# V of one pair of heads moved ahead of a weight tile and held until the first pair is normalised; the order of the early steps written out

## The chip, the cores and the metric

The kernel runs on one core of a Trainium2 chip. The metric is the device time of one execution in microseconds; several executions are timed and their median is given. One further execution is recorded by the hardware profiler; its trace gives the rows below, in microseconds from the start of its span.

The engines are named as in the profile: PE is TensorE, with its weight loads as PEld; DVE is VectorE, ACT is ScalarE, POOL is GpSimd, and SP is SyncE, which issues nearly all transfers.

## The reference

Attention with a local window and some global tokens feeds two MLP stages one after the other:

```python
def _attn_ref(q_l, k_l, v_l, q_g, k_g, v_g):          # (4, 8, 512 or 32, 64) each
    k_all, v_all = [concatenate of global and local]
    s_g = scale * q_g @ k_all^T ; out_g = sm(s_g) @ v_all
    s_ll = scale * q_l @ k_l^T, kept where |i - j| <= 32
    s_lg = scale * q_l @ k_g^T
    out_l = sm([s_lg, s_ll]) @ v_all
    return [out_g, out_l]

x = attention output as (2304, 512)
h = x @ w_in                                           # (512, 2048)
x = (h * clip(h + 3, 0, 6) / 6) @ w_out                # (2048, 512)
h = max(x @ w1, x @ w2, x @ w3)                        # (512, 768) each
out = h @ w_4                                          # (768, 512)
```

All of it is float32. The kernel makes each float32 product from three products of a rounded high part and a low part (`hi`, `lo`).

## The kernel before, in words

Attention is worked in 16 steps of one batch and one pair of heads (`pair(b, pr, s0)`, four batches by four pairs). For one pair the queue of SP loads Q, K and V (`qr`, `kr`, `vr`, three buffers each); TensorE makes the scores (L469), VectorE masks them and takes the row maximum (`rowmax`, L482), ScalarE takes exponentials (L488), TensorE turns them (`flip`, L512), and `pv` (L523) multiplies them with V. `norm` (L531) divides by the sums and writes the tile `ox`; TensorE turns it once more (`xflip`, L538), and ScalarE and VectorE write its high and low parts into `rx` (L550, L552). For every second pair `globals_` does the same for the global tokens (L576 scores, L587 row maximum, L607 flip, L620 product with V).

Beside this run the loads of w_in: 16 tiles of 512 KB go into a staging tile `raw` with two buffers (`decode`, L664). ScalarE and VectorE put the float32 bits together (L642 to L652), and ScalarE and POOL write the high and low parts (L668, L669). With these the first MLP stage, `first` (L695), starts as soon as x of the first two pieces of tokens is there; its tiles are stored to HBM by SP (`gstore`, L721). The second, third and fourth matrix products follow (L859, L983, L1138).

The order of the work on every engine is fixed when the program is built. Each step is an `op` with an engine, an estimated duration, a due time, the buffers it reads and writes, and at times an earliest time `rel`. `Plan.order` plays the steps through against these estimates and takes, on each engine, the ready step with the earliest due time; the instructions are issued in the order in which it took them. [...] In the list of before, SP's transfers around the change are: Q and K of the third pair; V of the second; w_in's first tile; Q and K of the fourth pair; w_in's second tile; V of the third pair; Q and K of the fifth pair; w_in's third tile.

A `Buf` is one use of a buffer, and `Plan.op` makes a step wait for every earlier step that touches the same `Buf` where one of them writes. V's load is issued by line 455 (`v` below). The lines that build the operands of the third product for the tokens "A" (`operands`, L1039) and the sums of the last stage (`double`, L1154) carry the other two due times that the change touches.

Of the kernel before, what the change touches and what calls it, by code (L numbers as in the profile page):

```python
# [33 lines left out]
TOK = {"A": (0, 256), "B": (512, 512), "C": (1536, 320)}  # L34
# [65 lines left out]
class Plan:  # L100
# [40 lines left out]
    def order(self):  # L141
# [4 lines left out]
        free, cand, out, pipe, port, form = {}, {}, [], 0.0, dict(DVE=0.0, POOL=0.0), "F"  # L146
# [22 lines left out]
        def elsewhere(o, e, t):  # L169
            mine = cost(o, e, t)  # L170
            return any(cost(o, x, begin(o, x)) < mine - (0.0 if x < e else 1e-6) for x in o.may if x != e)

        def begin(o, e):
# [18 lines left out]
                    t = max(t, max(u.done for u in old.users) + 0.1)  # L192
            return t

        while len(out) < len(self.ops):
            picks, wait, at = [], {}, {}
            for e, ops in cand.items():
                f = free.get(e, 0.0)
# [2 lines left out]
                    wait[e] = [(o.due, o.n, SHARE * o.may[e] if o.may else o.us) for t, _, o in at[e] if t <= f + LOOK]  # L201
            for e, ops in cand.items():
                ts = [(t, o) for t, b, o in at[e] if not (o.may and elsewhere(o, e, b))]
                if not ts:
                    continue
                if e == "PE":
                    ts = [(t + stall(o, t), o) for t, o in ts]
                t0 = min(t for t, _ in ts)
                stay = lambda o: e == "PE" and form != "F" and FORM.get(o.what) == form
                pick = min(((not stay(o), o.due, o.n, t, o) for t, o in ts if t <= t0 + WAIT), key=lambda x: x[:3])[1:]  # L210
                picks.append((pick[2], e != "-", pick[0], pick[1], pick[3], e))
            assert picks, "no step can start"
            t0 = min(picks)[0]
            t, _, _, _, o, e = min((p for p in picks if p[0] <= t0 + WAIT), key=lambda p: p[1:4])
# [43 lines left out]
                o.end = max([d.end for d in o.deps] + [t])  # L258
            o.done = o.end + (DRAIN if o.eng == "PE" else 0.0)
            cand[o.eng].remove(o)  # L260
            out.append(o)
            for s in o.succ:
                s.left -= 1
# [3 lines left out]
        return out  # L267


PLAN = []  # L270
WAIT = 0.02
RATE = 340.0
# [7 lines left out]
SPLIT = 2  # L280
LATE, SHARED = 2.473, 0.718
TS = "BC"
STEPS = (7.62, 8.87, 11.397, 7.881)
LAG = 124.236
W4DUE = 4
# [10 lines left out]
def body(ctx, tc, q_n, k_n, v_r, w_in, w_o, w_3, w_4, out):  # L296
# [144 lines left out]
    def pair(b, pr, s0):  # L441
# [7 lines left out]
        for n, (t, src, cut, size) in enumerate(((Q, q_n, 256, NQ + SG), (K, k_n, 448, NK))):  # L449
            for i, (a, z) in enumerate(((0, cut), (cut, size)) if first_ else ((0, size),)):  # L450
                e, issue = ("ACT", nc.scalar) if first_ and n else ("SP", nc.sync)
                op(e, 0.45, lambda t=t, src=src, a=a, z=z, issue=issue: issue.dma_start(
                    out=t()[:, a:z], in_=src[b, pr][:, a:z]), s0 - 7.919 + i, w=[(t, i)] if first_ else [t],
                   kb=(z - a) / 2, rel=s0 - 15.079, what="qk"[n])
        op("SP", 0.5, lambda: nc.sync.dma_start(out=V(), in_=v_r[b, pr]), s0 - 4.432 + 5 * first_, w=[V], kb=1024, rel=s0 - 2.826, what="v")

        TB, NM, OB = [Buf(T["t"]) for _ in range(2)], Buf(T["nm"]), Buf(T["o"])
# [67 lines left out]

        op("PE", 0.95, pv, s0 + 3.515, r=PT + [V], w=[OB], what="pv", ni=129)
        OX, XT = Buf(T["ox"]), Buf(T["s"])

        def norm():
            r = NM()[:, 2].rearrange("p i h -> p (i h)").rearrange("p (x o) -> p x o", o=1).to_broadcast([128, 8, D])  # L530
# [145 lines left out]
    def tt(e, out, a, b, f):  # L676
        ENG[e].tensor_tensor(out=out, in0=a, in1=b, op=f)  # L677
# [358 lines left out]
    yb = lambda p: lambda i: yv(p)[:, (1, 3, 0, 2)[i]]  # L1036
    yk = lambda p: [YK[p, i] for i in (1, 3, 0, 2)]
    S = {}
    S["A"] = operands(yb("A"), [Y["A"]], yk("A"), "sA", TOK["A"][1], TD - 14)  # L1039
    S["C"] = operands(yb("C"), [Y["C"]], yk("C"), "sC", TOK["C"][1], TD - 8)  # L1040
    plan.event(lambda: (fw_es.close(), re.open()), ("fw",), ("re",))
    S["B"] = operands(yb("B"), [Y["B"]], yk("B"), "sB", TOK["B"][1], TD + 8)
# [102 lines left out]
    def double(ts, due, t):  # L1145
# [5 lines left out]
                out=blk(2 - 2 * i, 2).rearrange("p (k m) -> p k m", k=NH), in_=hd[:, :, ts[i]:ts[i] + 128]),  # L1151
               t - 12, r=rows(ts[i]), w=[(W, 1 - i)], kb=560, what="hload")
        for o, x, y, f in ((4, 0, 1, ALU.add), (6, 2, 0, ALU.subtract), (5, 4, 2, ALU.subtract), (7, 3, 5, ALU.subtract)):
            op(both(384), dp(384), lambda e, o=o, x=x, y=y, f=f: tt(e, blk(o), blk(x), blk(y), f), t - 7, r=[key(x), key(y)], w=[key(o)],  # L1154
               what="wsum")
        for at, k in ((1, 3), (4, 4)):
            r = [key(i) for i in range(at, at + k)]
# [72 lines left out]
```

## Time and profile before

| | us |
|---|---|
| median of 3 runs | 712.08 |
| lowest, highest | 710.86, 712.6 |
| the profiled execution, device time | 708.55 |
| the profiled execution, span of its instructions | 706.8 |
| TensorE busy in that span | 693.6 |
| VectorE, ScalarE, POOL busy | 528.1, 380.0, 124.7 |

The profile is read from TensorE, which is busy nearly all the time: the list of its waits says where it is not, the table of windows says how busy each engine and the DMA engines are in a stretch and which clock TensorE was granted, and the timeline shows the instructions around one place. The time from 0 to about 160 us is attention with the first MLP stage beside it.

### The profile page before, as it was taken

Reading aid. Unit: us, or ns where it says so; the run is one execution under the profiler, and the core shown is the slowest. Engines: PE = TensorE matmul, PEld = TensorE weight load, DVE = VectorE, ACT = ScalarE, POOL = GpSimd, SP = SyncE. Lnnn points to the kernel's source line nnn. Section 1 sums busy time; section 2 is a strip of 40 time slices with the busy share of each in tenths; the row PEclk is TensorE's granted clock in tenths of the full one; section 3 lists DMA queues with packets and bytes.
Section 4 is the critical chain, followed back from the end, with each engine's and each line's share of the span. In section 5 each row is a group of like instructions: output and inputs, shape, how many; then the busy total and the mean of one; then the engine's idle time right before and its main releaser. Section 6 shows DMA issues by size and latency. Waiting matters only on the chain.

```text
span 706.8 us, 16042 instructions
## 1 busy us (share of the span) xinstructions
PE 693.6 (98%) x6380; PEld 617.2 (87%) x6380; DVE 528.1 (75%) x1117; ACT 380.0 (54%) x807; POOL 124.7 (18%) x161
## 2 busy tenths in 40 slices
PE   7899999999999999999999999999999999999998
PEld 5677888788888999988999998898999999898998
DVE  5798986657863565699867589998878876486980
ACT  6798886754432334565554366755444435154552
POOL 2136463200001352101010000011211320010100
PEclk9999999999999999999999999999999999999999
DMA  9689988716875766675576588001463471366632
GB/s 345 242 319 346 341 337 318 254 62 234 318 267 222 264 229 220 245 244 177 146 234 186 144 293 289 15 1 59 147 218 105 153 239 50 105 193 216 186 130 90
DMA packets 67003, 144.57 MB, mean 205 GB/s; under 512 B 4976, under 2 KB 35440, under 8 KB 63856
## 3 DMA queue, kind: packets, MB, share of 16 engines
q1 hardware_dynamic: 66640, 143.13, 58.6%
q8 instruction: 50, 0.82, 0.5%
q10 hardware_dynamic: 288, 0.41, 0.2%
q14 instruction: 25, 0.20, 0.1%
HBM read 98.04 MB, written 45.48 MB: 203 GB/s over the span
## 4 chain that ended last, share of the span: by engine, by line
PE 90%; DMA 3%; DVE 2%; ACT 2%; issue 1%; SPq 0%; POOL 0%; ACTq 0%; POOLq 0%
PE bank L983 34%; PE bank L695 25%; PE bank L859 22%; DMA kr<-in_kn_dram 2%; PE o L523 2%; PE bank L1138 2%; PE s L512 2%; PE s L469 1%; PE s L538 1%; PE s L620 1%; DMA fw<-gsC 1%; ACT t L488 1%; DMA raw<-in_w_in_dram 1%; PE s L576 1%; PE s L607 1%
## 5 line engine op out<-in xcount | busy, mean ns | idle before, releaser
L695 PE MATMUL bank<-rx,rw 128*128 128x512 f32 (+1 forms) x960 | 197.8, 362 | 0.5 <-DVE rx L552 0.2
L695 PEld LDWEIGHTS bank<-rx,rw 128*128 128x128 f32 x960 | 161.8, 188 | 23.5 <-issue 1.2
L859 PE MATMUL bank<-rr,rw 128*128 128x320 f32 (+2 forms) x912 | 154.7, 331 | 0.9 <-DVE rr L677 0.9
L859 PEld LDWEIGHTS bank<-rr,rw 128*128 128x128 f32 x912 | 140.3, 188 | 14.7 <-DVE rr L677 1.7
L983 PE MATMUL bank<-rw,rr 128*128 128x256 f32 (+2 forms) x648 | 100.0, 302 | 0.1
L983 PEld LDWEIGHTS bank<-rw,rr 128*128 128x128 f32 x648 | 90.5, 188 | 5.0 <-ACT rf L435 0.7
L782 ACT CAST rr<-fw 128x1024 fp32r<-128x1024 f32 (+2 forms) x76 | 62.1, 820 | 53.9 <-PE bank L859 46.3
L677 DVE TENSOR_TENSOR rr<-fw,rr 128x1024 fp32r<-128x1024 f32 (+2 forms) x76 | 72.6, 961 | 23.8 <-ACT rr L782 22.8
L705 ACT ACTIVATE rq<-bank,three 128x512 f32<-128x512 f32 (+1 forms) x60 | 37.9, 635 | 49.9 <-PE bank L695 41.8
L707 DVE SCALAR_TENSOR_TENSOR rq<-rq,bank 128x512 f32<-128x512 f32 (+1 forms) x60 | 36.8, 617 | 30.8 <-ACT rq L705 30.7
L435 ACT COPY rf<-bank 128x256 f32<-128x256 f32 (+2 forms) x72 | 32.9, 465 | 47.9 <-PE bank L983 37.4
L488 ACT ACTIVATE t<-t,nm 128x128 f32<-128x128 f32 x128 | 49.9, 392 | 12.3 <-DVE nm L482 12.1
L677 POOL TENSOR_TENSOR rq<-rq 128x256 f32<-128x256 f32 (+2 forms) x44 | 37.6, 855 | 106.2 <-DVE rq L677 83.1
L677 POOL TENSOR_TENSOR rf<-rf 128x256 f32<-128x256 f32 (+2 forms) x32 | 29.9, 950 | 143.5 <-DVE rf L677 44.2
L983 PE MATMUL bank<-re,rr 128*128 128x512 f32 x222 | 54.9, 391 | 0.0
L983 PE MATMUL bank<-rw,re 128*128 128x256 f32 (+2 forms) x369 | 53.8, 292 | 0.0
L983 PEld LDWEIGHTS bank<-rw,re 128*128 128x128 f32 x369 | 49.3, 188 | 1.6 <-DVE re L677 0.2
L1077 DVE TENSOR_TENSOR rf<-rf,bank 128x320 f32<-128x320 f32 (+2 forms) x72 | 37.0, 529 | 14.8 <-PE bank L983 13.4
L983 PEld LDWEIGHTS bank<-re,rr 128*128 128x128 f32 x222 | 40.7, 188 | 8.0
L482 DVE CUSTOM_DVE_ANT_0 t<-s,mask 128x128 f32<-128x128 f32 x116 | 26.5, 284 | 10.4 <-PE s L469 10.4
L677 DVE TENSOR_TENSOR rf<-rf 128x384 f32<-128x384 f32 (+4 forms) x56 | 30.9, 583 | 3.6 <-DMA rf<-hd 3.5
L677 DVE TENSOR_TENSOR re<-rf,re 128x1024 fp32r<-128x1024 f32 (+4 forms) x20 | 26.5, 1327 | 1.9 <-ACT re L1160 1.9
(134 smaller groups left out, 964.7 us busy)
## 6 DMA issues: line engine op xcount, KB each, us to landing
vr<-in_v_dram SPq DMA_DIRECT2D x16, 1024.0 KB, 7.3
fw<-gsB SPq DMA_DIRECT2D x28, 512.0 KB, 4.7
raw<-in_w_dram SPq DMA_DIRECT2D x24, 512.0 KB, 3.9
fw<-gsC SPq DMA_DIRECT2D x28, 320.0 KB, 3.4
raw<-in_w_in_dram SPq DMA_DIRECT2D x16, 512.0 KB, 5.3
raw<-in_w_o_dram SPq DMA_DIRECT2D x16, 512.0 KB, 4.4
fw<-gsA SPq DMA_DIRECT2D x28, 256.0 KB, 2.8
gsB<-rq SPq DMA_DIRECT2D x6, 1024.0 KB, 5.2
```

The source lines that it names most:

```text
L435: (nc.scalar.copy if eng == "ACT" else nc.vector.tensor_copy)(out=out, in_=in_)
L482: nc.vector.tensor_tensor_reduce(out=TB[hh]()[:, i], in0=SB[hh]()[:, 128 * i:128 * i + 128], in1=mask()[:, (i + 1) // 2 if i < 3 else 2], ...
L488: nc.scalar.activation(out=t, in_=t, func=ACTF.Exp, scale=-1.0, bias=NM()[:, 0, i, hh:hh + 1], accum_out=NM()[:, 1, i, hh:hh + 1])
L512: nc.tensor.transpose(FB()[:, 128 * i:128 * i + 128], TB[hh]()[:, i], ident)
L677: ENG[e].tensor_tensor(out=out, in0=a, in1=b, op=f)
L695: nc.tensor.matmul(ps()[:, 0:m], lhsT=w[:, i, k], rhs=xs(c)[:, j, k], start=(k == 0 and s == 0), stop=(k == KC - 1 and s == 2))
L705: op("ACT", us, lambda ps=ps, m=m, out=out: nc.scalar.activation(out=out(), in_=ps()[:, 0:m], func=ACTF.Relu, bias=three), -100, r=[ps], w ...
L707: op("DVE", us, lambda ps=ps, m=m, out=out: nc.vector.scalar_tensor_tensor(out=out(), in0=out(), scalar=6.0, in1=ps()[:, 0:m], op0=ALU.min ...
L782: op("ACT", act(n) + 0.01, lambda: nc.scalar.copy(out=out(0), in_=src()), due, r=r, w=[(w, "hi")], what=what + "_hi")
L859: nc.tensor.matmul(A[e]()[:, 0:n], lhsT=w[:, 2 * fp + f, u, e], rhs=r[:, v, f], start=(seed is None and fp + f + s == 0), stop=(fp == 3 an ...
L983: nc.tensor.matmul(bank()[:, 0:n], lhsT=w[:, u, k], rhs=r[:, v, k], start=(start and k + s == 0), stop=(k == K - 1 and s == 2), skip_group ...
L1077: op("DVE", dve(n), lambda q=q, src=src, mv=mv: nc.vector.tensor_tensor(out=mv(q)(), in0=mv(q)(), in1=src(), op=ALU.max), -200, r=[bank], ...
```

## The change

V of the third pair (batch 0, pair 2) moves ahead of w_in's second tile in SP's order. Before it stands a new step on POOL, "hold": it copies one column of the first pair's normalised tile `ox` into the first column of that V's buffer. The load of V writes the same buffer, so it waits for the copy, and the copy waits for the first pair's `norm`.

The order of the first 312 steps of TensorE and the first 117 of SP is no longer chosen by due time but given as a list, `SEQ`, of step numbers (a step's number is its place in the order in which the code creates the steps). The other engines are still ordered by `Plan.order`. Against the order of before, the lists hold the same steps; neighbours change places in many spots. Among them: the first pair's two halves of Q (7 before 6), K ahead of Q for the fifth and some later pairs, the third pair's `xflip` ahead of the first `first` step, and the scores that ran at 58.32 before behind four further steps. The due times of the "A" operands and of the last stage's sums move by 4 and 2 us in the planner's time.

```diff
@@ Plan.order
+        turn = {e: list(seq) for e, seq in SEQ.items()}
...
             for e, ops in cand.items():
                 ts = [(t, o) for t, b, o in at[e] if not (o.may and elsewhere(o, e, b))]
+                if turn.get(e):
+                    ts = [(t, o) for t, o in ts if o.n == turn[e][0]]
...
             cand[o.eng].remove(o)
+            if turn.get(o.eng):
+                turn[o.eng].pop(0)
...
+SEQ = dict(
+    PE=(2, 0, 3, 1, 5, 4, 11, 12, 21, 44, 32, 73, 76, 34, 63, 36, 65, 94, 81, 38, 67, 83, 113, 69, 85, 441, 444, 87,
+        115, 125, 117, 119, 265, 266, 144, 412, 271, 267, 146, 272, 273, 148, 431, 433, 449, 451, 150, 461, 453, 268,
...
+    SP=(7, 6, 41, 42, 10, 90, 91, 43, 153, 122, 123, 93, 160, 410, 409, 167, 124, 174, 458, 459, 181, 411, 188, 490,
...
+HOLD = {2: 0}
...
@@ pair
+        if b == 0 and pr in HOLD:
+            was = held[0, HOLD[pr]]["OX"]
+            op("POOL", 0.07, lambda: nc.gpsimd.tensor_copy(out=V()[:, 0, 0, 0:1], in_=was()[:, 0:1]), -100, r=[was], w=[V], what="hold")
         op("SP", 0.5, lambda: nc.sync.dma_start(out=V(), in_=v_r[b, pr]), s0 - 4.432 + 5 * first_, w=[V], kb=1024, rel=s0 - 2.826, what="v")
...
         OX, XT = Buf(T["ox"]), Buf(T["s"])
+        S["OX"] = OX
...
-    S["A"] = operands(yb("A"), [Y["A"]], yk("A"), "sA", TOK["A"][1], TD - 14)
+    S["A"] = operands(yb("A"), [Y["A"]], yk("A"), "sA", TOK["A"][1], TD - 10)
...
@@ double
-            op(both(384), dp(384), lambda e, o=o, x=x, y=y, f=f: tt(e, blk(o), blk(x), blk(y), f), t - 7, r=[key(x), key(y)], w=[key(o)],
+            op(both(384), dp(384), lambda e, o=o, x=x, y=y, f=f: tt(e, blk(o), blk(x), blk(y), f), t - 9, r=[key(x), key(y)], w=[key(o)],
                what="wsum")
```

In the list of SP, 93 is V of the third pair, 160 is w_in's second tile, and 410 and 409 are K and Q of the fifth pair.

## Rows read from the trace of the kernel before

**Rows 1.** The page, part 1: busy us, share of the span, instructions.

```profile
span 706.8 us, 16042 instructions
...
PE 693.6 (98%) x6380; PEld 617.2 (87%) x6380; DVE 528.1 (75%) x1117; ACT 380.0 (54%) x807; POOL 124.7 (18%) x161
```

**Rows 2.** Waits of TensorE, whole span: us in total, times, longest.

```profile
PE s L469 <- DMA kr<-in_kn_dram: 3.1, 3, 1.5
PE o L523 <- issue: 2.9, 2, 2.4
...
PE bank L859 <- DVE rr L677: 0.9, 3, 0.5
PE s L620 <- issue: 0.7, 1, 0.7
```

**Rows 3.** Windows: length, busy PE PEld DVE ACT POOL, granted clock, DMA share, GB/s.

```profile
18.00:20.00 2.00, 0.00 (x0) 0.00 (x0) 0.10 (x1) 2.00 (x10) 0.00 (x0) 0.91 0.98 399
20.00:22.00 2.00, 1.84 (x21) 1.66 (x22) 1.13 (x4) 0.03 (x1) 0.00 (x0) 0.50 0.85 324
22.00:24.00 2.00, 2.00 (x56) 1.58 (x56) 1.03 (x3) 0.86 (x3) 0.00 (x0) 0.73 0.14 53
24.00:26.00 2.00, 1.96 (x19) 1.28 (x17) 1.99 (x7) 1.94 (x7) 0.20 (x1) 1.00 0.00 0
```

**Rows 4.** Timeline, PE: start, us, line, tiles, count, [idle before, releaser].

```profile
13.94 0.30 PE L523 MATMUL o<-vr,pt 128*32 128x64 f32 x2 [0.47 <-issue]
...
16.82 0.91 PE L523 MATMUL o<-vr,pt 128*32 128x64 f32 x49
20.16 0.65 PE L523 MATMUL o<-vr,pt 128*32 128x64 f32 x15 [2.43 <-issue]
...
26.30 1.10 PE L469 MATMUL s<-kr,qr 64*32 64x96 f32 x62 [0.33 <-DVE g L587]
...
28.35 0.73 PE L695 MATMUL bank<-rx,rw 128*128 128x512 f32 x2
...
30.01 0.66 PE L538 MATMUL s<-ident,ox 128*128 128x128 f32 x4 [0.21 <-DVE ox L531]
```

**Rows 5.** DMA queue "instruction", 17.60:17.80, then 21.40:21.60: packets, MB, share of 16 engines.

```profile
q8 instruction: 1, 0.02, 34.2%
...
q8 instruction: 1, 0.02, 31.2%
```

**Rows 6.** Timeline, SP's queue: when transfers were issued.

```profile
11.57 1.41 SPq L664 DMA_DIRECT2D raw<-in_w_in_dram  x1
13.03 0.43 SPq L455 DMA_DIRECT2D vr<-in_v_dram  x1
...
26.92 0.33 SPq L664 DMA_DIRECT2D raw<-in_w_in_dram  x1
```

**Rows 7.** Tile raw: issue to landing of w_in's first (4.85), then third tile (26.92).

```profile
DMA to landing us min/median/max: 11.5/11.5/11.5
...
DMA to landing us min/median/max: 3.8/3.8/3.8
```

**Rows 8.** Timeline, DVE, POOL and ACT around the first and second pair.

```profile
14.28 0.69 DVE L531 TENSOR_TENSOR ox<-o,nm 128x512 f32<-128x512 f32 x1 [0.96 <-PE o L523]
14.32 0.19 POOL L595 TENSOR_TENSOR g<-g,small 128x1 f32<-128x1 f32 x1 [1.26 <-ACT tg L593]
17.02 0.21 POOL L562 MEMSET tg<- 128x128 f32 x1 [2.50 <-PE s L607]
24.02 1.24 ACT L646 ACTIVATE rq<-raw 128x512 f32<-128x512 f32 x2
```

**Rows 9.** Timeline, PE: scores that waited for K, and the next flip.

```profile
7.94 1.10 PE L469 MATMUL s<-kr,qr 64*32 64x96 f32 x64 [1.52 <-DMA kr<-in_kn_dram]
...
58.32 1.10 PE L469 MATMUL s<-kr,qr 64*32 64x96 f32 x64 [1.32 <-DMA kr<-in_kn_dram]
...
60.15 0.60 PE L512 MATMUL s<-ident,t 128*128 128x128 f32 x4
```

18 rows, old and new, of tables (PE, SP) are left out of this document.

## Prediction

> **What bounds the kernel now.** The page first: TensorE is busy for 693.6 of 706.8 us [rows 1]. So the end comes earlier only where TensorE's idle time, or time at a lower clock, disappears. The list of its waits comes next: hardly anything but K tiles that land late (3.1 us), 0.9 us behind splits for the second MLP stage, and two entries "issue", 2.9 and 0.7 us, in which it waited for nothing that has a semaphore [rows 2]. The long one stands in the timeline of TensorE: the second pair's `pv` stops after 49 matmuls at 17.73 and goes on at 20.16; the first pair's had stopped after 62 of 64, for 0.47 us [rows 4]. Between the two stops lie six rows with 2 + 4 + 64 + 4 + 4 + 49 = 127 matmuls, each with its weight load: 254 instructions. The queue named "instruction" moves packets of 0.02 MB; one starts at 17.6 to 17.8, another at 21.4 to 21.6 [rows 5]. I read this as TensorE's own code arriving block by block, the next block being asked for when a block is entered. The packet at 17.7 was then asked for at 13.94 (3.7 us of queueing), and matmuls ran on 2.5 us after it began. The one at 21.5 was asked for at 20.16 (1.3 us).
>
> The windows show what it queued behind and what the stop cost: the DMA engines are full until about 22.0 (0.85 of 20 to 22, 0.14 of 22 to 24, none of 24 to 26), and the granted clock is 0.50 and 0.73 in the two windows after the stop, against 1.00 from 24 [rows 3]. So the load on the DMA engines is 8.0 us deep at 13.94 and 1.8 us at 20.16. The line through the two points is: queueing = 1.3 + 0.39 x (depth - 1.8).
>
> **The change part by part.** *The hold.* POOL gets one copy of 128x1. The nearest row, an addition of that shape, took 0.19 us. The copy waits for the first pair's `norm`, which ends at 14.28 + 0.69 = 14.97, so it ends near 15.2, and V of the third pair is issued near 15.3 instead of 13.03 [rows 6, 8]. Behind the copy on POOL stands the memset of `tg`, which starts at 17.02, when TensorE's global flip releases it [rows 8]: nothing is delayed. Behind V on SP stand, in the new list, w_in's second tile (11.57 before; near 15.8 now) and then K and Q of the fifth pair, which followed V before as well (from 13.56 to near 16.3) [rows 6]. So four transfers, 1024 + 512 + 400 + 288 KB = 2.28 MB, are no longer queued at 13.94. At 399 GB/s [rows 3] that is 5.7 us of depth: 2.3 instead of 8.0. Queueing is then 1.5 us, the packet starts at 15.4, before the held transfers bring data, and matmuls can go on at 17.9 against a stop at 17.73: a stall of **0.2 instead of 2.43 us, 2.2 gained**.
>
> *The clock.* [...] TensorE was busy 1.84 us at 0.50 and 2.00 us at 0.73 [rows 3]; at 1.00 the same work takes 0.92 and 1.46, so 3.84 - 2.38 = **1.46 gained**. The ends of this term are nothing (the clock falls anyway) and 1.46; I take the upper one, since the same rows show 1.00 wherever no such stop came before.
>
> *What is late next.* After 20.16 TensorE runs into VectorE, which has to go from the second pair's `norm` through the second `g_rowmax` (L587) before the fourth pair's scores go on at 26.30 [rows 4]. VectorE idles in 18 to 24 (0.10, 1.13, 1.03 us busy of 2 each [rows 3]), so it can start as much earlier as TensorE does: 2.2 + 1.46 = **3.65 us** at 26.3, which puts that point at 22.65. The next code block: entered at 17.9 with 2.28 MB issued at 15.3 to 16.7. w_in's third tile, issued at 26.92 into an idle queue, landed after 3.8 us [rows 6, 7], 1.3 of which are its 0.52 MB at 399 GB/s; half of the other 2.5 lies before its data, so I let the held data flow from 16.5. At 17.9 0.6 MB of it is through, 4.2 us are left, queueing is 1.3 + 0.39 x 2.4 = 2.2, and the code is there at 17.9 + 2.2 + 2.5 = 22.6. It is needed 127 matmuls further on; the nine rows from 20.16 to 25.61 hold 92, so that is 35 matmuls into the row at 26.30, about 26.9 before and 23.3 now [rows 4, 5]. No new stall, with 0.7 us to spare.
>
> *Who needs the held tiles.* The third pair's `pv` ran at 27.3, the fifth pair's scores later still; issued near 15.3 and 16.3 they land by 23 to 24. The second w_in tile was first read in ScalarE's row at 24.02 (its second instruction, 24.6) [rows 8]. The tile took 3.8 us to land into an empty queue (the third tile) and 11.5 us behind two V (the first) [rows 7]; mine has one V of 2.6 us ahead of it: 15.8 + 3.8 + 2.6 = 22.2. In the shifted timeline it is wanted from 21 on; ScalarE and VectorE have other steps to put there, since their order follows the planner's own times. I take 0, and 2.6 us at worst (below).
>
> *The written list.* It holds the first 312 TensorE and 117 SP steps; compared with the order before, it swaps neighbours. Four swaps have a row. (1) The first pair's Q comes second half first, so the first scores start up to 0.45 us (one issue) later; the cover is the wait of 1.52 us for the second pair's K at 7.94 [rows 9]; cost 0, without the cover 0.45. (2) The third pair's transposition follows its `pv` directly; before, `first` matmuls stood between, from 28.35 to 30.01, and it still waited 0.21 us for VectorE [rows 4]. Between 0 and 30.01 - 28.35 - 0.21 = 1.4 us lost; I take **0.4 lost**, nearer to 0, since VectorE and not TensorE is full there and the skipped work can be done as soon as its weights are decoded. (3) The scores that waited 1.32 us for K at 58.32 go behind one `first` step, a flip and two global flips [rows 9]. The gain is at most 1.3; that flip ran at 60.15, 1.8 us after the scores, so as much can be lost too. I take 0. (4) Halves of `first` and loads change places up to 150 us; the second code stall, 0.7 us [rows 2], can go or come again: 0, plus or minus 0.75.
>
> *The two due times* (A's operands 4 us later, the sums of the last stage 2 us earlier in the planner's ranking): no wait of TensorE after the second MLP stage's 0.9 us is listed [rows 2]. So nothing can be gained; a reordered operand could cost, bounded by a wait of the length listed, 0.5. I take 0.
>
> **Sum.** 2.2 + 1.46 - 0.4 = 3.2 us. From the early stage on TensorE is filled, so the shift reaches the end. The profiled execution, 708.55, would be 705.3; the median of the runs is 712.08, 3.5 above it, and the same shift gives **708.9**. The forecast's own range: 3.65 + 1.3 + 0.75 less nothing gives 706.4; 2.2 - 1.4 - 0.45 gives 711.7.
>
> **Rivals.** *A: the stall moves.* The held transfers crowd the next code block instead. With the full depth of 5.7 us in front, queueing is 2.8 and not 2.2, which the 0.7 us still cover; beyond that each microsecond that the code is late is a microsecond of stop. At the 3.7 us of queueing that the first deep queue showed, the code is there at 24.1, 0.8 late, and if the clock falls behind this stop as it did before, the 1.46 is gone too: 3.2 - 0.8 - 1.46 = 0.9 gained, **711.2**. For: 2.28 MB now lies together. Against: the margin worked out above.
>
> *B: the stop is not made by the queue.* If code waits for one packet in its way at most, emptying the queue gives nothing: **712.1**. For: the first stop, 0.47 us, came with a deep queue too. Against: 3.7 against 1.3 us in two rows that differ in depth.
>
> [...]
>
> *C: slower.* w_in's second tile comes too late. Place: ScalarE's scale of the second tile and VectorE's steps behind it, which stand in order before the fourth pair's rowmax. If the tile takes the first tile's 11.5 us [rows 7] from 15.8, it lands at 27.3, 2.7 us after its first read before, and the whole early stage hangs on it: 712.1 + 2.6 = **714.7**. It decides against the change from a landing after about 24.6; up to there the gain only shrinks. Against: fewer bytes lie ahead of it than of the first tile.
>
> **Chances.** Forecast 0.58, A 0.15, B 0.13, C 0.14. What a measurement of this kernel can tell from no change is about 0.3%, 2.1 us, so faster means below 709.9. Of the forecast 0.50 lies there and 0.08 within; of A 0.03 and 0.12; B is within; of C 0.13 is slower, 0.01 within. Faster 0.53, same 0.34, slower 0.13. The range from 706.3 to 712.5 holds the forecast's own ends, A and B, with the runs' scatter of about 0.4 beyond B, and leaves C out.
>
> **What would show it.** In the profile of after: V of the third pair issued near 15.3, the second w_in tile right behind it; the "instruction" packet near 15.4; the second pair's `pv` with no stop over 0.5 us; a granted clock of 1.00 from 18 to 24; the fourth pair's scores near 22.7; no "issue" wait near 23; and the remaining timeline shifted by some 3 us. Wrong if the packet still starts near 17.6 (B), if a stop of 1 us or more stands near 23 (A), or if ScalarE or VectorE waits for `raw` before 25 (C).

## The result, and the profile after

The changed kernel took 714.57 us (median of 6 runs, 713.32 to 715.85) against 712.19 of the kernel before in the same comparison (6 runs): a ratio of 1.0054, 95% interval 1.0029 to 1.0078, so slower by half a per cent. Run again, instruction for instruction the same, it gave 1.0077 (1.005 to 1.0103). The forecast was 708.9 us, between 706.3 and 712.5.

Line numbers of the changed kernel are higher by 28 to 32: the scores L469 are L500 there, `flip` L512 is L543, `pv` L523 is L554, `xflip` L538 is L570, `first` L695 is L727. The page of the changed kernel, part 1, to hold against [rows 1]:

```profile
span 712.9 us, 16035 instructions
...
PE 698.1 (98%) x6380; PEld 616.4 (86%) x6380; DVE 531.5 (75%) x1109; ACT 381.6 (54%) x811; POOL 130.1 (18%) x166
```

The early part went as forecast. TensorE's timeline, changed kernel, for [rows 4]:

```profile
14.38 1.41 PE L554 MATMUL o<-vr,pt 128*32 128x64 f32 x64
...
18.36 1.43 PE L554 MATMUL o<-vr,pt 128*32 128x64 f32 x64
...
24.53 1.56 PE L500 MATMUL s<-kr,qr 64*32 64x96 f32 x62 [0.16 <-DVE g L619]
26.02 1.10 PE L554 MATMUL o<-vr,pt 128*32 128x64 f32 x64
27.97 0.66 PE L570 MATMUL s<-ident,ox 128*128 128x128 f32 x4 [0.85 <-DVE ox L563]
```

Both `pv` run through, 64 matmuls each with no stop. The second starts 1.54 us later than before and the fourth pair's scores go on 1.77 us earlier: 3.31 us are gained in between, where 3.65 were forecast. The head of this execution, which the change hardly touches, was the slower one (last section). The hold and what it lets go, in the timelines of POOL and SP, for [rows 6]:

```profile
16.61 0.18 POOL L485 COPY vr<-ox 128x1 f32<-128x1 f32 x1 [0.25 <-DVE ox L563]
```

```profile
16.82 0.33 SPq L486 DMA_DIRECT2D vr<-in_v_dram  x1
17.20 1.11 SPq L696 DMA_DIRECT2D raw<-in_w_in_dram  x1
```

And the windows, for [rows 3], with the granted clock at 1.00 in all of them:

```profile
18.00:20.00 2.00, 1.91 (x71) 1.49 (x70) 2.00 (x14) 2.00 (x10) 0.21 (x1) 1.00 0.79 302
20.00:22.00 2.00, 1.74 (x50) 1.33 (x52) 1.72 (x4) 2.00 (x8) 0.00 (x0) 1.00 0.97 387
22.00:24.00 2.00, 2.00 (x41) 1.46 (x29) 1.84 (x6) 1.40 (x6) 0.20 (x1) 1.00 1.01 391
```

The loss comes later. These are the times in the timelines at which the `pv` of some of the 16 pairs starts, and the end of the span. "Before again" and "hold alone" are runs of the next section.

| us | pair 2 | 3 | 5 | 8 | 9 | 10 | 16 | span |
|---|---|---|---|---|---|---|---|---|
| before | 16.82 | 27.32 | 42.81 | 74.01 | 83.47 | 94.91 | 151.81 | 706.8 |
| before again | 18.05 | 29.31 | 45.58 | 76.55 | 86.01 | 97.49 | 155.67 | 710.0 |
| hold alone (second run) | 17.48 | 24.87 | 41.32 | 71.33 | 80.79 | 92.23 | 151.51 | 705.4 |
| changed | 18.36 | 26.02 | 43.13 | 73.46 | 87.62 | 101.64 | 158.06 | 712.9 |
| changed again | 18.82 | 26.23 | 44.79 | 72.17 | 85.98 | 99.96 | 156.41 | 710.8 |

Against before, the changed kernel is 1.3 us ahead at the third pair, 0.3 behind at the fifth and 6.2 behind at the last; 6.1 are left at the end. Against before again it is 2.4 behind at the last and 2.9 at the end, near the 2.4 us between the medians; the first profile of before is a quick execution. (The marks of the second and third pair have the same matmuls before them in both orders. In the list the eighth has 73 fewer before it, the fifth 8, the ninth 44 and the last 48 more, so these marks are off by some 3 us one way and 1 or 2 the other; the end is not.) From the last mark to the end all five take 553.9 to 555.0 us, so the loss lies before it. The waits of TensorE from 40 to 100 us, first before, then changed:

```profile
PE s L469 <- DMA kr<-in_kn_dram: 1.3, 1, 1.3
PE bank L695 <- DVE rx L552: 0.2, 1, 0.2
```

```profile
PE s L570 <- DVE g L619: 1.5, 1, 1.5
PE s L660 <- DVE gx L657: 0.9, 1, 0.9
PE s L652 <- ACT pt L463: 0.8, 1, 0.8
PE s L543 <- ACT t L519: 0.8, 1, 0.8
PE s L543 <- DVE nm L513: 0.5, 1, 0.5
PE o L554 <- DVE pt L463: 0.5, 1, 0.5
PE s L500 <- DVE rx L584: 0.4, 1, 0.4
PE bank L727 <- DVE rq L739: 0.2, 1, 0.2
```

That is 1.5 us against 5.6 us (2.0 in before again; 4.6 in changed again, 1.5 of them a stop marked "issue" at 43.99), and the kind has changed: one late K before, eight places at which TensorE stands in front of a step whose VectorE or ScalarE input is not ready. In windows of 20 us TensorE is busy 18.24 and 18.29 where it was busy 20.00 and 20.00 before (19.16 and 20.00 in before again). Before, then changed:

```profile
60.00:80.00 20.00, 20.00 (x333) 16.18 (x332) 17.42 (x62) 18.09 (x55) 10.74 (x14) 1.00 0.97 344
80.00:100.00 20.00, 20.00 (x393) 16.31 (x392) 17.24 (x63) 16.65 (x51) 10.63 (x15) 1.00 0.87 317
...
60.00:80.00 20.00, 18.24 (x373) 13.67 (x372) 15.96 (x61) 14.15 (x46) 8.75 (x11) 1.00 0.80 273
80.00:100.00 20.00, 18.29 (x324) 14.40 (x323) 17.93 (x62) 16.86 (x53) 11.90 (x15) 1.00 0.83 308
```

A second trace of the same thing lies on SP. Its longest wait of 45 to 100 us for POOL's sums, before and changed:

```profile
SPq L721 <- POOL rq L677: 5.3, 2, 3.2
```

```profile
SPq L753 <- POOL rq L709: 14.2, 3, 7.2
```

For 7.2 us SP stands in front of one store, and a w_in tile, the next store, Q, K and V stand behind it. The DMA engines run empty meanwhile (0.25 and 0.03 of 70 to 74, against 0.91 and 0.86 before), and VectorE, which before never waited for w_in in this stretch, now does. Changed kernel, windows and VectorE's waits:

```profile
70.00:72.00 2.00, 2.00 (x14) 1.69 (x12) 1.63 (x7) 1.98 (x7) 1.39 (x3) 1.00 0.25 102
72.00:74.00 2.00, 1.77 (x21) 1.05 (x19) 1.84 (x5) 1.42 (x3) 1.45 (x2) 1.00 0.03 12
```

```profile
DVE raw L676 <- DMA raw<-in_w_in_dram: 3.3, 3, 1.7
```

### The profile page after: what moved, and what is told of

It is laid out like the page before. It is cut to its first block, busy times and chain, and to the rows that moved or that the text cites. A ratio compares the mean times of both kernels' runs of the same rounds, so it can differ in the third digit from the quotient of the medians.

```text
span 712.9 us, 16035 instructions
## 1 busy us (share of the span) xinstructions
PE 698.1 (98%) x6380; PEld 616.4 (86%) x6380; DVE 531.5 (75%) x1109; ACT 381.6 (54%) x811; POOL 130.1 (18%) x166
## 4 chain that ended last, share of the span: by engine, by line
PE 87%; DMA 5%; DVE 4%; ACT 3%; issue 1%; SPq 0%; ACTq 0%
PE bank L1015 33%; PE bank L727 24%; PE bank L891 21%; DMA raw<-in_w_in_dram 3%; PE bank L1170 2%; PE s L500 1%; PE s L543 1%; PE o L554 1%; ACT t L519 1%; PE s L608 1%; DMA fw<-gsC 1%; DMA kr<-in_kn_dram 1%; DVE t L513 1%; DVE raw L676 1%; PE s L570 1%; DVE rr L709 1%
## 5 line engine op out<-in xcount | busy, mean ns | idle before, releaser
L727 PE MATMUL bank<-rx,rw 128*128 128x512 f32 (+1 forms) x960 | 201.3, 363 | 0.4 <-DVE rq L739 0.2
L727 PEld LDWEIGHTS bank<-rx,rw 128*128 128x128 f32 x960 | 161.0, 188 | 23.0 <-issue 1.3
L709 DVE TENSOR_TENSOR rr<-fw,rr 128x1024 fp32r<-128x1024 f32 (+2 forms) x76 | 74.1, 979 | 24.2 <-ACT rr L814 23.2
L709 POOL TENSOR_TENSOR rq<-rq 128x256 f32<-128x256 f32 (+2 forms) x45 | 39.1, 868 | 106.9 <-DMA gsB<-rq 64.3
L709 POOL TENSOR_TENSOR rf<-rf 128x256 f32<-128x256 f32 (+1 forms) x34 | 31.0, 925 | 136.9 <-DMA w4d<-rf 51.0
L1109 DVE TENSOR_TENSOR rf<-rf,bank 128x256 f32<-128x256 f32 (+2 forms) x72 | 37.0, 529 | 14.6 <-PE bank L1015 13.6
L1015 PE MATMUL bank<-rr 128*128 128x320 f32 (+1 forms) x174 | 27.1, 303 | 0.0
```

What stands on the lines that cost most here:

```text
L727: nc.tensor.matmul(ps()[:, 0:m], lhsT=w[:, i, k], rhs=xs(c)[:, j, k], start=(k == 0 and s == 0), stop=(k == KC - 1 and s == 2))
L1015: nc.tensor.matmul(bank()[:, 0:n], lhsT=w[:, u, k], rhs=r[:, v, k], start=(start and k + s == 0), stop=(k == K - 1 and s == 2), skip_group ...
L1109: op("DVE", dve(n), lambda q=q, src=src, mv=mv: nc.vector.tensor_tensor(out=mv(q)(), in0=mv(q)(), in1=src(), op=ALU.max), -200, r=[bank], ...
```

## The experiments

Most of them change one thing in the kernel before. So that nothing else moves, the order that each engine had is written down for all five engines and `Plan.order` only takes the head of each list:

```diff
-                ts = [(t, o) for t, b, o in at[e] if not (o.may and elsewhere(o, e, b))]
+                ts = [(t, o) for t, b, o in at[e] if (o.n == turn[e][0] if turn.get(e) else not (o.may and elsewhere(o, e, b)))]
```

Numbers in the lists are step numbers; where the hold is in, they are higher by one from 92 on, since it is a step itself. Ratios are to the kernel before on the same chip, with a 95% interval, from five rounds.

**The scatter of the method.** The kernel before with its own order written down; no instruction differs.

> The kernel before once more, with the order of every engine written out as the planner had it, so the same instructions. It gives a second profile of the kernel before and the scatter of a comparison in which nothing differs: within 0.3%, with the stop of about 2.4 us in the second pair's pv; the granted clock in the first 20 us may differ from the first profile's.

Ratio 0.9986 (0.996 to 1.0011), span 710.0 us. So a comparison of a kernel with itself can come out 0.14% off, and the two comparisons of the changed kernel lie 0.23% apart. The profiled execution from which the prediction was worked (706.8) was a quick one: this one lies 3.2 us above it.

**The hold alone.** Order of before on all engines, with the copy on POOL and V ahead of the tile.

```diff
-    SP=(... 153, 122, 123, 160, 93, ...)   POOL=(... 61, 79, 440, ...)
+    SP=(... 153, 122, 123, 93, 160, ...)   POOL=(... 61, 79, 92, 440, ...)
```

> The hold and the move of V alone: every engine keeps the order of the kernel before; only the hold's copy on POOL is added, and the third pair's V stands ahead of w_in's second tile. Theory (the hold pays, the written list costs): V is issued near 15.3, the second pair's pv stops for under 0.5 us instead of 2.43, the granted clock stays at 1.00 from 18 to 24, and the time is 2.2 to 3.6 us below the kernel before: near 709. Rival (the hold itself costs, since w_in's second tile and K and Q of the fifth pair come 4 us later): the stop goes, but ScalarE or VectorE waits for raw or TensorE for K between 20 and 60, and the time is equal to the kernel before or up to 3 us above it.

> The hold and the move of V alone, a second time, since the first comparison (0.9983, from 0.9959 to 1.0007) could not tell a gain of 3 us from none. If the gain is what the profile of the first run showed, the ratio is near 0.996 and the lead over the second profile of the kernel before is about 3 us by 25 us; if the profile was a lucky execution, the ratio is within 0.2% of 1.

Ratios 0.9983 (0.9959 to 1.0007) and 0.9963 (0.9943 to 0.9983), spans 703.4 and 705.4. Only the second tells a gain from none, and the kernel before against itself, in the same comparison as the second, gave 0.9986. TensorE's timeline in the second run:

```profile
17.48 1.18 PE L523 MATMUL o<-vr,pt 128*32 128x64 f32 x64
...
23.31 0.79 PE L469 MATMUL s<-kr,qr 64*32 64x96 f32 x35 [0.33 <-DVE g L587]
24.30 0.64 PE L469 MATMUL s<-kr,qr 64*32 64x128 f32 x27 [0.21 <-issue]
```

No stop in `pv`; from it to the fourth pair's scores 5.83 us instead of 9.48, which is 3.65 gained, the forecast's figure. The next stop marked "issue", 0.21 us, comes 35 matmuls into the scores, where the prediction had placed the next code block.

The hold also has a price, which the ratios already contain. ScalarE stood 0.51 and 0.57 us, in the two runs, in front of its first read of w_in's second tile; its timeline, second run:

```profile
22.70 0.67 ACT L646 ACTIVATE rq<-raw 128x512 f32<-128x512 f32 x1 [0.57 <-DMA raw<-in_w_in_dram]
```

And TensorE waited for V tiles, 0.9 and 1.4 us in all (in the second run 0.81 at 41.32 and 0.64 at 104.09), where it waited for none before and 0.2 in before again.

**The hold, V staying behind the tile.** Only the copy on POOL is added.

> The kernel before with the hold, but V of the third pair stays behind w_in's second tile; all else as before. If the gain comes from emptying the queue ahead of TensorE's code, V with K and Q behind it (1.7 of the 2.3 MB) is enough: the second pair's pv stops for 0.3 to 0.8 us instead of 2.43, and the time is 1.5 to 3 us below the kernel before. If it comes from V standing ahead of the tile, nothing is gained.

Ratio 0.9984 (0.9964 to 1.0005), span 707.1. The ratio does not tell it from the first run above; the timeline does, since both stops are there:

```profile
14.05 0.30 PE L523 MATMUL o<-vr,pt 128*32 128x64 f32 x2 [1.40 <-issue]
...
20.00 0.43 PE L523 MATMUL o<-vr,pt 128*32 128x64 f32 x15 [2.15 <-issue]
```

So it was not enough to take V out of the queue. With the tile still ahead, issued at 10.75, the stop was 2.15 us; with the tile held back too, in the two runs above, there was none.

**The hold and one swap.** As the hold alone, with one `first` step ahead of the eighth pair's scores (TensorE `541, 302` to `302, 541`).

> The hold and the move of V, and on TensorE one first step (three matmuls of 0.23 us) moved ahead of the eighth pair's scores, which wait for K near 57. Theory: the step fills 0.7 us of that wait, so the time is 0.7 us below the hold alone and 2 to 4 us below the kernel before. Rival: the scores come later by what the step takes beyond the wait; no difference from the hold alone.

Ratio 0.9961 (0.9942 to 0.9981), span 703.8: no different from the hold alone. In this execution the head was quicker, TensorE went on behind its first stop at 13.54 with the DMA engines still full of earlier loads (busy share 1.03 of 13 to 15, 1.10 of 15 to 16), the packet of the queue "instruction" came between 16.2 and 16.4, and part of the stop came back:

```profile
18.66 0.43 PE L523 MATMUL o<-vr,pt 128*32 128x64 f32 x15 [1.33 <-issue]
```

**The first pair's Q halves alone.** SP `6, 7` to `7, 6`.

> The kernel before with the first pair's two halves of Q issued in the other order, and nothing else. Theory (the late first scores keep TensorE at the lower clock): the first scores start near 4.8 instead of 4.0, the granted clock first stands at 1.00 near 13.7 instead of 6.0, the second pair's scores take 1.9 us instead of 1.1, and the time rises by 1 to 1.6 us. Rival (the cover that the prediction named, the wait for the second pair's K at 7.94, holds): the time rises by less than 0.3 us.

Ratio 1.0007 (0.9978 to 1.0036): no cost is seen, as in the prediction. The interval still holds the 1 to 1.6 us (0.14 to 0.23%) of the theory that I formed on seeing the result (a later first Q keeps the clock low in the head), and two of its signs are in this profile: the first scores start at 4.67, and the second pair's take 1.95 us. But these take 1.95 us in before again too, with Q in the old order. And over all profiled executions the first pair's `pv` starts at 12.0 to 15.1 us with the halves exchanged (eight, 13.6 on average) and at 11.4 to 14.9 without (twelve, 13.4). So the theory finds no support. Nor is the clock of the head a property of the kernel: between 6 and 14 us it was 1.00 throughout in one profile of before, and 0.50 in 9 to 11 in the other.

**The list alone.** Both lists, other engines ordered by `Plan.order`; no hold, Q, V and the due times as before.

> The kernel before with the written list for TensorE and SP, but with the first pair's Q in the order of before, V of the third pair where it stood, no hold, and the due times of before. The planner orders ScalarE, VectorE and POOL around the list, as in the changed kernel. Theory (the list costs): TensorE idles some 3 us more than before between 40 and 100 us, behind VectorE, and the time is 3 to 5 us above the kernel before. Rival (the list is neutral and the rest of the change costs): within 1 us of the kernel before.

Ratio 1.0093 (1.0063 to 1.0124). TensorE's timeline:

```profile
73.67 0.32 PE L523 MATMUL o<-vr,pt 128*32 128x64 f32 x8 [1.31 <-ACT pt L435]
74.96 1.72 PE L523 MATMUL o<-vr,pt 128*32 128x64 f32 x56 [0.97 <-ACT pt L435]
```

This is where the forecast fell: 0.93% is 6.6 us, not 0.4. The two stops shown are 2.3 of them, and behind them the granted clock falls to 0.50 (in the window from 76 to 78), so that the next scores take 1.84 us instead of 1.10. The other waits from 40 to 100 us add up to 1.9.

**SP's list alone** (other engines as before) and **TensorE's list alone** (SP as before, the other three by `Plan.order`).

> The kernel before with SP's part of the written list alone (the first pair's Q and the third pair's V in their old places, no hold, old due times); the other engines keep the order of before. The list puts K of the ninth pair ahead of a store and a w_in tile and its Q behind that tile. Theory (SP's list is a good part of the loss, since a transfer that waits for a free buffer holds up the Q behind it): TensorE waits for qr or kr near 65 to 70, and the time is 2 to 5 us above the kernel before. Rival (the loss is TensorE's list): within 1 us of the kernel before.

> The kernel before with TensorE's part of the written list alone; SP keeps the order of before, ScalarE, VectorE and POOL are ordered by the planner around it. Theory (TensorE's list is the loss, because steps that wait for VectorE or ScalarE stand ahead of work that is ready): TensorE idles 2 us or more in excess of before between 40 and 100 us; the time is 3 to 6 us above the kernel before. Rival (SP's list is the loss): within 1 us.

Ratios 1.0041 (1.0018 to 1.0064) and 1.011 (1.0088 to 1.0131). With SP's list one new wait of TensorE stands out, and the clock falls behind it (0.50 from 72 to 74; these scores take 1.95 us instead of 1.10):

```profile
71.97 1.95 PE L469 MATMUL s<-kr,qr 64*32 64x96 f32 x64 [2.08 <-DVE rx L552]
```

The chain of waits leads back from there over VectorE, POOL's guard and POOL's sums to the landing of a store that SP had issued at 60.75. It is not the late Q that I had expected. With TensorE's list the waits are spread (whole span):

```profile
...
PE s L512 <- ACT t L488: 2.8, 5, 1.0
...
PE s L538 <- DVE ox L531: 1.6, 1, 1.6
PE bank L695 <- DVE fw L707: 1.2, 1, 1.2
PE s L469 <- DVE pt L435: 1.2, 1, 1.2
...
```

In this run and in the list alone `Plan.order` also gave VectorE, ScalarE and POOL a new order. No run puts TensorE's whole list together with their old orders, so what part of the loss is the list's own and what part is that of the orders made around it is not shown.

**Two swaps by themselves**, all engines otherwise as before: the eighth pair's scores behind `first`, flip, two global flips and `first` (`540, 301, 512, 528, 530, 302` to `301, 512, 528, 530, 302, 540`), and the third pair's `xflip` directly behind its `pv` (`116, 264, 118` to `116, 118, 264`).

> The kernel before with one swap of TensorE's written list alone: the eighth pair's scores behind a first step, a flip, two global flips and another first step. The prediction put this between 1.3 us gained and 1.8 lost and took 0. Theory (a step that waits for ScalarE ahead of the scores delays VectorE's row maxima and so the next pairs): TensorE waits in front of that flip, the scores start 2 to 4 us later than before, and the time rises by 1.5 to 4 us. Rival (the swap fills the wait for K): the time falls by up to 1 us.

> The kernel before, all engines in its own order, with one swap on TensorE: the third pair's transposition stands directly behind its pv, ahead of the first step that stood between them. Theory: TensorE waits for VectorE's norm with nothing to do, 1.1 to 1.6 us as in the kernel with TensorE's list alone and in the changed one, and keeps it: 1.0015 to 1.0022. Rival (the prediction's term): 0.4 us, 1.0006, since the skipped work only comes later; or nothing, if VectorE's order is what counts: 1.0.

Ratios 1.0031 (1.0008 to 1.0055) and 1.0036 (1.0006 to 1.0066), some 2.2 and 2.5 us with wide intervals. The first price rests on the times alone: TensorE's waits from 40 to 100 us add up to 1.1 us in it, against 1.5 before. In the second the wait is seen directly; it was 0.21 us in [rows 4]:

```profile
30.19 0.66 PE L538 MATMUL s<-ident,ox 128*128 128x128 f32 x4 [1.59 <-DVE ox L531]
```

**The first of these put back in the changed kernel** (`541` ahead of `302`; the other engines by `Plan.order`).

> The changed kernel with one step of TensorE's written list put back to where the order of before had it: the eighth pair's scores before one first step, the flip, the two global flips and a further first step, not behind them. Theory: the swap cost 0.31% when it was made alone, and undoing it gives that back: 1.002 of before, with the scores starting near 60 and not at 61.36. Rival: the planner orders ScalarE, VectorE and POOL anew around any list, and the other waits of the list stay: 1.0054, within its interval.

Ratio 1.0078 (1.0048 to 1.0108). Nothing came back, so its price alone is not its price here. With one step moved, VectorE's and ScalarE's orders change too, and other waits grow (2.4 us for `t`, 1.6 for `pt`).

**The due times alone, and put back in the changed kernel** (`TD - 14` to `TD - 10`, `t - 7` to `t - 9`, and the reverse).

> The kernel before with the two due times alone (A's operands 4 us later, the last stage's sums 2 us earlier). Theory: A's operands come late and TensorE waits 0.7 us at the start of the third product near 455 to 460; the time rises by 0.5 to 1 us. Rival (the prediction's 0): no wait there beyond those of the kernel before, and no difference that can be measured.

> The changed kernel with the two due times of before. Theory (the due times cost by themselves, 0.64% in the run alone, but most of what they cost depends on the order around them): the changed kernel's waits near 425 to 460 go, and the time is 0.5 to 2 us below the changed kernel, so 2 to 3.5 us above the kernel before. If their price is the same as in the run alone, the time is level with the kernel before.

Alone 1.0064 (1.0035 to 1.0093). Two new waits stand in the third product, which had none there before, and TensorE is busy 18.48 of 480 to 500 us instead of 19.91:

```profile
PE bank L983 <- DVE rr L677: 1.4, 1, 1.4
PE bank L983 <- DVE rw L677: 0.4, 2, 0.2
```

Up to 440 us every engine works in the order of before here, so what the due times cost must lie behind that. From the last pair's `pv` to the end this execution took 557.3 us, against 555.0 and 554.3 in the two of before: 2.3 to 3.0 us, or 0.3 to 0.4%, at the low end of the interval.

Put back: 1.004 (1.0021 to 1.0059), against 1.0054 and 1.0077 with them, so 0.1 to 0.4% by the times, not resolved. From the last pair's `pv` to the end it took 554.2 us, against 554.8 and 554.4 in the changed kernel: 0.2 to 0.6 us.

**The changed kernel without the hold** (list and due times kept).

> The changed kernel without the copy on POOL that holds V of the third pair back; the written list (V ahead of w_in's second tile) and the two due times stay. Theory: the hold is worth the same inside the list as it was with the order of before, 0.17 to 0.37%, so this kernel is slower than the changed one by that: 1.0071 to 1.0091 of before, a stop near 18 in the second pair's pv of 2 us or more, granted clock below 1.00 behind it. Rival: TensorE runs into VectorE and ScalarE later in the list anyway, and the early gain is used up there: 1.0054, as the changed kernel, with the stop back.

Ratio 1.0068 (1.0045 to 1.009), not told from the changed kernel by time. The stop is back, longer than in [rows 4], but the clock did not fall behind it. TensorE's timeline, then the windows:

```profile
20.97 0.43 PE L554 MATMUL o<-vr,pt 128*32 128x64 f32 x15 [2.97 <-issue]
```

```profile
20.00:22.00 2.00, 1.03 (x21) 0.89 (x21) 0.55 (x1) 0.29 (x2) 0.00 (x0) 1.00 0.83 318
22.00:24.00 2.00, 1.99 (x60) 1.50 (x60) 1.56 (x4) 1.11 (x4) 0.05 (x1) 1.00 0.19 66
```

**POOL's sums first in the changed kernel**: the last two token sums of one group, then of all eight, directly behind the first two, and the changed kernel again with nothing moved.

```diff
-    POOL=(... 296, 297, 558, 298, 222, 299, ...)
+    POOL=(... 296, 297, 298, 299, 558, 222, ...)
```

> The changed kernel, every engine in the order that the changed kernel had, with one change on POOL: the last two token sums of one group of columns (they ran at 70.77 and 72.72) stand directly behind the first two (65.88), ahead of the guard that waited 3.18 us for ScalarE and of a split. Theory: SP's queue stood from 66.2 to 73.47 because the store of those sums waited for POOL, and a w_in tile, the next store, Q and K stood behind it; the DMA engines' hole from 70 to 74, VectorE's 3.3 us of waiting for w_in tiles and part of TensorE's idle time between 60 and 100 (3.47 us more than before) come from that. Then the store is issued near 68.5, SP's wait on POOL falls from 14.2 to about 9 us, the hole is filled, and 1 to 3 us come back: 1.001 to 1.004 of before. Rival: TensorE is held up by VectorE and ScalarE themselves, whose order is the planner's, and the tile is not what VectorE is late by: the store moves, TensorE's idle time stays, 1.0054.

> As the run before this one, for the last two token sums of all eight groups of the first stage. Theory: what the first such move gives back, and somewhat more, since SP waits for POOL's sums three times (14.2 us in all) between 45 and 100: 1.0 to 1.003. Rival: 1.0054, as the changed kernel; or slower, since splits of later w_in tiles now stand behind sums.

> The changed kernel again, instruction for instruction, with each engine's order given: what two comparisons of the same instructions differ by on the side of the changed kernel. 1.0054 is expected by every theory, give or take the 0.14% by which the kernel before, run again, differed from itself.

Ratios 1.0034 (1.0015 to 1.0053), 1.0061 (1.0042 to 1.0081) and 1.0077 (1.005 to 1.0103). With one group moved, the store leaves at 67.73 instead of 73.47, the hole closes, and TensorE is full again from 80 to 100, though not from 60 to 80 (18.36):

```profile
80.00:100.00 20.00, 20.00 (x393) 15.96 (x392) 18.21 (x65) 17.87 (x54) 10.99 (x16) 1.00 0.77 265
70.00:72.00 2.00, 2.00 (x16) 1.40 (x14) 2.00 (x8) 1.64 (x3) 1.22 (x1) 1.00 0.84 287
72.00:74.00 2.00, 1.47 (x74) 1.09 (x80) 1.53 (x5) 1.39 (x3) 0.43 (x1) 1.00 0.80 253
```

With all groups moved the hole is closed as well (0.96 and 0.88), but one wait behind VectorE that the first variant lost is back, at 93.61:

```profile
PE s L570 <- DVE g L619: 1.5, 1, 1.5
```

Only the first variant can be told from the changed kernel, and only from its run in the same comparison (1.0034 against 1.0077, not against 1.0054). So SP's stand is not the cause by itself. My reading, which these runs support but do not prove, is that it makes VectorE late, and that what costs is a step of TensorE's fixed order that meets a late VectorE; which step that is changes with every small reordering.

## Why the prediction was wrong

*The stall, 2.2 us: right.* The copy, V right behind it, the tile right behind V and `pv` without a stop all came as forecast, in the changed kernel and in the hold alone. V was issued at 16.82 instead of near 15.3 because the head of this execution was slower; in the second run of the hold alone it was issued at 16.09 and the "instruction" packet came between 15.8 and 16.0, where 15.4 was forecast. Rival B falls as it was stated: the eleven profiled executions with V and the tile in the way, or the tile alone, stopped for 2.0 to 3.0 us in the second `pv`. Of the nine with V and the tile held back five ran through and four stopped for 0.5 to 1.4 us, the longer ones where the head was quick. In three of these stops (before, the hold with V behind the tile, the hold with one swap) matmuls went on 2.3 to 2.6 us after that packet began (17.76, 17.4 to 17.6, 16.2 to 16.4), as the 2.5 read from one row had it. My line through two points, queueing against bytes in front, is refuted as a formula: with V held and the tile ahead it put the stop at 0.7 us, and 2.15 were measured.

*The clock, 1.46 us: only half the time.* I took the fall of the clock as an effect of the stop. Of the eleven executions that stopped for 2 us or more at that place, the granted clock fell to 0.50 behind the stop in six (both runs of before, Q halves, SP's list, hold in place, scores late) and stayed at 1.00 in five (list alone, due times, TensorE's list, no hold, `xflip` first). None of the nine others shows a lower clock there. From the end of the stop to the fourth pair's scores TensorE took 6.1 to 6.5 us where the clock fell (five of the six; the other has no separate row) and 4.9 to 5.2 where it stayed, so the size was about right at 1.2. The term is there in some executions and 0 in others, 6/11 of 1.46 or about 0.8 on average. I had given both ends and took the upper one on a single execution.

*What is late next, 3.65 us at the fourth pair's scores: right in size* (3.31 and 3.65 measured). At the end less of it is left: 0.17% and 0.37%, 1.2 and 2.6 us, with a scatter of 0.14% or more; the waits for V tiles in the hold alone, 0.9 and 1.4 us, are part of the difference. In the table the second run is 2.7 us ahead of the first profile of before at the eighth pair and 1.4 at the end, and 4.6 ahead of the second profile at the end.

*Rivals A and C.* A was seen as 0.21 us in the hold alone and as 0.38 in two variants of the changed kernel, no more. C's sign was seen in the hold alone, ScalarE's 0.51 and 0.57 us for the second w_in tile before 25 us, at a small part of the 2.6 that C priced and without a stop of TensorE; the changed kernel does not show it. The tile came near 22.6 there, where I had 22.2. The slower result came from elsewhere, and no rival named it.

*The written list, 0.4 us lost: the step that failed.* The list alone costs 6.6 us. I had priced four swaps one at a time and let all others go at 0 ± 0.75. The second was to cost between 0 and 1.4; TensorE's wait there grew by 1.38, the upper end (0.64 in the changed kernel). The third I put at 0 with 1.8 at worst; it measured 2.2 alone. (The list puts those scores behind five steps, not four as I had counted: a second `first` step follows the global flips.) The first was 0, as said. The second code stall, a stop marked "issue" of 0.75 us at 140.77 before, was gone in the changed kernel; when that was run again, one of 1.46 us stood at another place, 43.99. But the larger error is in the form of the sum. It treated a swap as a move inside a fixed timeline. Here TensorE and SP take a new order, and `Plan.order` orders VectorE, ScalarE and POOL anew around it by its own estimates. How busy these are in the stage with most of the swaps I had not asked, beyond one place in the second swap. Over the whole span the trace of before shows VectorE at 75% and ScalarE at 54% [rows 1], which looks like slack. The window of that stage says otherwise (kernel before; busy PE, PEld, DVE, ACT, POOL):

```profile
40.00:100.00 60.00, 58.43 (x1141) 46.72 (x1124) 52.49 (x187) 52.40 (x159) 31.15 (x39) 1.00 0.91 326
```

VectorE and ScalarE are both busy 87% of it and the DMA engines 91%. There a step of TensorE that comes earlier than its input turned into a wait (5.6 us against 1.5), and so did a load behind a late store (7.2 us of SP).

*The due times, 0: wrong alone (0.64%), small in the changed kernel.* "No wait is listed" shows that nothing can be gained; it does not bound what can be lost. I had taken a listed wait's length, 0.5, as the upper end, and 1.4 and 0.4 us came. The time lost behind 440 us is 2.3 to 3.0 us alone and 0.2 to 0.6 in the changed kernel, whose orders with and without them part at 418 us.

*The sum.* Hold -0.17 to -0.37%, list +0.93%, due times +0.64%: these add up to +1.2 to 1.4%, and 0.54 and 0.77% were measured. With the due times at what they cost inside the changed kernel, 0.03 to 0.08%, the sum is +0.6 to 0.8%, which agrees. So the list explains the slower result; that is worked out from single profiles, and the intervals of the parts are some 0.3% wide to either side. What stays open is which of the list's many swaps make up its price: the scores' swap put back gave nothing, and POOL's sums moved ahead gave about half of the loss back in one form and nothing that can be told in the other.

*The base.* The rows came from a quick execution: 706.8 us, where the second profile of before shows 710.0. The forecast itself was set off from the median, so this did not make the miss; it made single rows, the fallen clock above all, look like properties of the kernel.

The version to keep is the hold with V ahead of the tile and the order of before: 0.9963 and 0.9983, and 0.9961 with one `first` step moved. Its second comparison and the one with the step moved are the only ones whose whole interval lies below the kernel before, by little more than the scatter; the hold with V left behind the tile (0.9984) cannot be told from either.

## What to carry to other kernels

A change that replaces a planner's order by a list is not a set of swaps with prices. Read the busiest of the engines that feed the one in fixed order, in windows of that stage and not over the span; where they are as busy as VectorE and ScalarE were here from 40 to 100 us, 87% against 75% and 54% over the span, count every step that comes earlier as a wait until a run shows otherwise. Take such a list apart from the idea that it comes with, and time the idea in the old order first.

## What the runs showed of the hardware

Behind a stop of TensorE of 2.0 to 3.0 us in the second `pv` the granted clock fell to 0.50 in six executions and stayed at 1.00 in five: it was 0.50 in the window from 20 to 22 of the kernel before, behind 2.43 us, and 1.00 behind the stop of 2.97 us of the changed kernel without the hold. In the head the granted clock differed between executions of the same instructions: the second pair's 64 scores took 1.10 us in before [rows 9] and 1.95 in before again, whose granted clock was 0.50 there, and the first pair's `pv` started at 12.26 and 14.25, of which 0.8 us is a later K.

There the windows and the matmuls can also disagree. From 8 to 13 us the windows give 1.00 for the changed kernel and 0.50 when it was run again, yet these scores took the same time in both. TensorE's timeline, changed, then changed again:

```profile
8.16 1.95 PE L500 MATMUL s<-kr,qr 64*32 64x96 f32 x64 [0.64 <-DMA kr<-in_kn_dram]
...
8.48 1.95 PE L500 MATMUL s<-kr,qr 64*32 64x96 f32 x64 [2.28 <-DMA kr<-in_kn_dram]
```

So in the first microseconds I would hold the window's figure against the length of known matmuls, here these scores with their 1.10 and 1.95 us.

The page of before has this line for the queue of TensorE's code, as the prediction read it:

```profile
q8 instruction: 50, 0.82, 0.5%
```

That is one packet for about 255 of TensorE's 12760 matmuls and weight loads [rows 1]. The three stops marked "issue" in before, 0.47, 2.43 and 0.75 us, ended 2.3 to 2.4 us after such a packet had begun (11.65 and 13.94, 17.76 and 20.16, 138.36 and 140.77).

With V and the tile ahead of it, the packet began 3.7 us after TensorE had gone on behind the first 62 matmuls of the first pair's `pv` (13.94 and 17.6 to 17.8, before). With both held back, in the second run of the hold alone, it began about 1 us after that place (14.7 and 15.8 to 16.0), and the second pair's `pv` ran through.
